# One maximum row per query, unmatched queries as a row product, the mean of V on TensorE: an attention stage rearranged

## The chip, the cores and the metric

The kernel runs on one core of one Trainium2 chip. The metric is the device time of one launch in microseconds (us). Three runs of the kernel before gave 839.99, 841.4 and 837.2 us, median 839.99. A core has five engines with a queue of instructions each: TensorE (PE: matmuls; PEld: the loads of their stationary operands, called weights here), VectorE (DVE), ScalarE (ACT), GpSimd (POOL) and SyncE (SP), which here only issues transfers (DMAs). Each works its own queue in order, and engines wait for each other by semaphores.

## The reference

Three layers follow each other: an attention in which a query sees only the keys of its own hash bucket, a gated feed-forward layer, and eight experts. The change touches the first alone, apart from the order in which the second one's first steps come.

```python
def _attn_ref(q, k, v, proj):                     # q, k, v: 2 x 8 heads x 768 x 64, proj: 64 x 6
    scale = 1.0 / np.sqrt(D)
    q_bits = (np.einsum('bhsd,dk->bhsk', q, proj) > 0)      # 6 bits: the bucket
    k_bits = (np.einsum('bhsd,dk->bhsk', k, proj) > 0)
    mask = q_bucket[:, :, :, None] == k_bucket[:, :, None, :]
    scores = scale * np.matmul(q, k.transpose(0, 1, 3, 2))
    scores = np.where(mask, scores, -1000000000.0)
    scores = scores - np.max(scores, axis=-1, keepdims=True)
    attn = np.exp(scores)
    attn = attn / (np.sum(attn, axis=-1, keepdims=True) + 1e-09)
    return np.matmul(attn, v)
# then, on 1536 tokens x 512:
#   first layer:  xn = rms_norm(x); (silu(xn @ w_gate) * (xn @ w_val)) @ w_out       (1536 hidden columns)
#   second layer: the expert of the largest logit, relu(x @ w1[e]) @ w2[e], times two gates
```

A query without any key in its bucket has 768 equal scores, so its output is the mean of V over the sequence.

## The kernel before

**Tiling.** The 16 heads are worked in 8 pairs. A pair's q and k are loaded (`load_qk`), transposed by TensorE (`prep_t`), split into a leading part and a rest (`prep_hi`, `prep_lo`), and multiplied by the projection for the bucket bits (`bits_dots`, `bits_mask`). SyncE copies these pieces inside SBUF into the operands `T` of a head (`place`: part 0 the leading parts, part 1 the bit rows, part 2 the rests). The bit rows are extra rows of the contraction: they put a penalty of 2^30 (`PEN`) on a key of another bucket.

**Per head.** The 768 queries are six tiles of 128, and so are the keys.
- `smax` (tile `psm`, L576): masked scores of 128 queries against all keys, two matmuls of 384 columns. `smax_red` (L585, VectorE) reduces them to one maximum per query.
- `setm` turns the maxima of a head into a row of `T`: to 0 where the query has no match (L597), split into a leading part and a rest (L600, L602), transposed (L605), copied out (L608), and sent into two rows of `T` by a DMA (L611). So the next product already has the maximum subtracted.
- `scores` (`pss`, L621): 128 keys against all queries, four matmuls. `exps` (L629, ScalarE) writes `Pe` in float32; `exps_lo` (L640) makes `Pl`, what is left of it beyond its upper half word, on GpSimd or, for the tiles listed in `PLV`, on VectorE.
- `pv` (`po`, L655, L656): output of 128 queries, twelve pairs of a weight load and a matmul: for each key tile the upper half of `Pe` against [leading V | 1 | rest of V | 0], 130 columns, and `Pl` against the first 65 of them. V is scaled by a power of two and split per head by `v_hi` (ScalarE) and `v_lo` (L506, VectorE).
- `pv_red` (L663, VectorE) adds the two halves of `po`; `head_out` makes the denominator (L673) and its reciprocal (L677) on VectorE and, on GpSimd, the mean of V where a query is unmatched (`u` L589, L680), the scaling (L684) and their sum (L686).

**Mean of V.** `mean_red` (L700, VectorE) adds the six tokens of a partition, `mean_dots` (L736, TensorE) the partitions; `abs_sum` (L705) and `v_scale` find the power of two.

**What sets the order.** `Plan` writes the order of every engine before the kernel starts: each step is added with an engine, a duration in ns, what it needs, a place (a number from tables such as `PT`, `SM`, `LATE`) and buffers; a model of the engines starts, of the steps that can run, the one with the least place. Two `P` (exponentials of a head) and three `S` (score tiles in PSUM) are there. The feed-forward layer has a `Plan` of its own behind it; its first norm and first weights (`n0` to `n5`, `w0`) are steps of the attention's plan.

Of the kernel before, what the change touches and what calls it, by code (L numbers as in the profile page):

```python
# [32 lines left out]
PT = ((-26.2, 3.87, 20.05, 19.0, 13.9), (-59.0, -88.6, -21.21, 8.39, 33.83), (1.61, -13.88, 4.9, -16.2, -30.33), (-0.8, -11.52, 5.11, -27.98, -8.39), (-1.86, -21.15, -8.14, -41.78, 8.93))  # L33
PD = (68.86, 49.56, -49.64, -53.27, 14.34)
SM = ((-25.22, 2.38, -4.9, 2.26), (-3.98, 1.69, 1.66, 1.07), (-2.41, 1.13, 7.87, 0.73), (-0.14, 1.24, 9.29, 0.52), (2.7, 1.02, -7.12, 11.99))
SV = (-51.83, 11.07, 7.09, 5.16, 12.58)
LQ = (3.84, 74.35, 127.92, 164.5, 49.05)
LV = (11.15, -49.62, -114.49, -63.86, -39.46)
TINY = 2.0 ** -126
TDA = (4,)  # L40
PLV = ((6, 11), (2, 11), (3, 6, 8), (4, 7), (0, 1, 3, 4, 5, 8, 9, 11))
PV0, PV1 = 10.03, 4.39
VAT = (-156.17, -11.57)
MVT = (-17.05, -173.85)
MLT = (131.86, 57.75)
NX, NW = 350.58, 20.18
CONST = 4.79
N0, N1 = 68.31, 14.5
LATE = {'tc': -15.85, 'td': 7.02, 'pr': 25.66, 'p0': -15.14, 'bi': -15.81, 'sx': 12.56, 'mk': -1.88, 'ex': 6.16, 'pl': -8.9, 'xr': 20.85, 'ho': -22.34, 'u': -63.48, 'sc': -1.81, 'sm': -2.37, 'pv': 48.28, 'vs': 27.89, 'tl': 14.99}


class Plan:
    """An order for a fixed set of steps: on each engine, of the steps that can run, the one with the least place."""
# [18 lines left out]

    def order(self):
        """Starts of the steps on a model of the engines: ns of each step, ns to its followers, buffers in use."""
# [8 lines left out]
        start, events, now, dma, done = {}, [], 0, 0, 0  # L83
# [10 lines left out]
        while True:  # L94
            for e, r in enumerate(ready):
# [10 lines left out]
                end = free[e] = now + steps[n][1]  # L106
# [33 lines left out]
def kernel(  # L140
# [85 lines left out]
    def constants():  # L226
# [6 lines left out]
        # per token: one, and the token's row of the output  # L233
# [15 lines left out]
    def x_tiles(w):  # L249
        """Leading parts and rests of w columns of activations, in two buffers by turns."""  # L250
# [7 lines left out]
    def to_psum(pt, src):  # L258
        """Token-major src [P, DM] transposed."""
# [20 lines left out]
    def norm_rsqrt(pool, d):  # L280
        """Steps from the sums of squares d["ss"] to d["ri"]: 1 / sqrt, from the exponent's bits by Newton's steps."""
# [59 lines left out]
    def convert(f, kind):  # L341
        """Steps from float64 words to float32: rebias the exponent, join the fraction's words, put the sign back."""
# [50 lines left out]
    def attention(ctx, after):  # L393
# [35 lines left out]
        MV = [tp.tile([P, DM], F32, name=f"MV{b}") for b in range(B)]  # L429
# [3 lines left out]
        VS = [tp.tile([P, 2, NT, 2, D + 1], F16, name=f"VS{i}") for i in range(2)]  # L433
        one128 = tp.tile([1, P], F32, name="one128")
# [46 lines left out]

        def ends_V(i):
# [992 lines left out]
```

## Time and profile before

| | |
|---|---|
| median of 3 runs | 839.99 us |
| span of the profiled execution (the page gives no other time of it) | 840.8 us |
| TensorE busy | 750.0 us, 89% |
| VectorE busy | 526.9 us, 63% |
| ScalarE busy | 380.7 us, 45% |
| GpSimd busy | 439.0 us, 52% |
| first and last scores start | 39.2 and 260.6 us |
| first matmul of the feed-forward layer | 273.3 us |

The span is the time from the first to the last instruction. A busy share is an average over three layers with different limits, so the stage matters: the attention fills the first 273 us, then the feed-forward layer's first chunk runs together with the conversion of its float64 weights until about 395 us, and the rest is matmuls almost without a break. An instruction of VectorE or GpSimd counts as busy also while it waits inside for a port. The granted clock of TensorE is given as a share of its 2.4 GHz.

### The profile page before, as it was taken

What the parts mean: (1) busy time and instruction counts of PE and PEld (TensorE: products, weight loads), DVE (VectorE), ACT (ScalarE), POOL (GpSimd) and SP (SyncE); (2) the same over time, 40 slices, a digit from 0 to 9 for tenths busy, and PEclk for the clock granted to TensorE, in tenths of its full rate; (3) what the DMA queues carried; (4) which work ended last, traced back from release to release, by engine and by line L of the source; (5) the groups of instructions that cost most, each with busy time, mean ns of one, the idle gap of its engine ahead of it and who ended that gap; (6) DMA issues with size and microseconds to landing.
All of it is one profiled execution on the core that took longest, in us unless ns stands there. A gap on an engine that the chain in (4) does not pass through costs nothing.

```text
span 840.8 us, 12945 instructions
## 1 busy us (share of the span) xinstructions
PE 750.0 (89%) x4722; PEld 629.8 (75%) x4722; DVE 526.9 (63%) x915; ACT 380.7 (45%) x625; POOL 439.0 (52%) x373
## 2 busy tenths in 40 slices
PE   5689898997887988879999999999987999999995
PEld 4368687876776666657878888788866888898984
DVE  5799998999998999998351222521243444455441
ACT  2066544543354544453443334434232666565662
POOL 4075676786569544444434444346116665655552
PEclk9599999999898999999999999999986999999998
DMA  7999767553501445440100001010038997767100
GB/s 148 190 227 215 166 129 154 121 120 62 137 1 51 151 155 165 143 145 18 51 1 0 1 1 51 1 38 13 1 126 256 340 334 212 220 204 188 39 23 19
DMA packets 101665, 97.03 MB, mean 115 GB/s; under 512 B 33501, under 2 KB 82845, under 8 KB 101600
## 3 DMA queue, kind: packets, MB, share of 16 engines
q1 hardware_dynamic: 98880, 88.84, 40.4%
q0 software_dynamic: 2560, 7.34, 2.5%
q8 instruction: 38, 0.62, 0.3%
q14 instruction: 27, 0.22, 0.1%
q10 hardware_dynamic: 160, 0.00, 0.0%
HBM read 69.50 MB, written 7.36 MB: 91 GB/s over the span
## 4 chain that ended last, share of the span: by engine, by line
PE 60%; DVE 29%; issue 5%; DMA 2%; SPq 1%; ACT 1%; POOL 0%; POOLq 0%; DVEq 0%; ACTq 0%
PE pg L915 16%; PE pg L1310 10%; PE pss L621 4%; DVE hm L362 4%; PE psm L576 3%; PE po L1324 3%; PE po L1323 3%; PE po L1322 3%; DVE m L585 3%; PE po L957 3%; PE po L959 3%; PE po L958 3%; PE po L655 2%; DVE Pl L640 2%; PE pt L261 1%
## 5 line engine op out<-in xcount | busy, mean ns | idle before, releaser
L640 POOL TENSOR_TENSOR Pl<-Pe 128x768 f16<-128x768 f32 x73 | 113.3, 1563 | 63.1 <-ACT Pe L629 59.1
L629 ACT ACTIVATE Pe<-pss,ebias 128x768 f32<-128x768 f32 x96 | 84.8, 902 | 109.1 <-PE pss L621 95.3
L378 POOL TENSOR_TENSOR wgl<-r,wgh 128x512 fp32r<-128x512 f32 x64 | 83.7, 1314 | 82.6 <-ACT wgh L388 80.9
L585 DVE TENSOR_REDUCE m<-psm 128x1 f32<-128x768 f32 x96 | 89.4, 948 | 14.2 <-PE psm L576 12.9
L621 PE MATMUL pss<-T 128*128 128x384 f32 x384 | 89.1, 363 | 9.3 <-DVE m L585 4.2
L937 DVE TENSOR_TENSOR si<-pg,si 128x512 f32<-128x512 f32 x36 | 24.8, 688 | 109.8 <-PE pg L915 109.8
L928 POOL TENSOR_TENSOR wgl<-wy_g,wgh 128x512 fp32r<-128x512 f32 x35 | 47.5, 1356 | 80.0 <-ACT wgh L388 80.0
L621 PEld LDWEIGHTS pss<-T 128*128 128x128 f32 x384 | 69.0, 199 | 13.5 <-DVE m L585 5.5
L378 DVE TENSOR_TENSOR wvl<-r,wvh 128x512 fp32r<-128x512 f32 x64 | 47.2, 737 | 47.9 <-ACT wvh L388 42.0
L1310 PE MATMUL pg<-xh,wgh 128*128 128x256 f32 x256 | 73.5, 288 | 0.7 <-ACT xh L264 0.7
L928 POOL TENSOR_TENSOR wol<-wy_o,woh 128x512 fp32r<-128x512 f32 x36 | 49.0, 1364 | 47.8 <-ACT woh L388 45.1
L928 POOL TENSOR_TENSOR wvl<-wy_v,wvh 128x512 fp32r<-128x512 f32 x35 | 48.1, 1375 | 49.1 <-ACT wvh L388 46.0
L1310 PE MATMUL pg<-xl,wgh 128*128 128x256 f32 x256 | 72.7, 284 | 0.0
L1310 PE MATMUL pg<-xh,wgl 128*128 128x256 f32 x256 | 72.6, 284 | 0.0
L655 PE MATMUL po<-VS,Pe 128*128 128x130 f16 x576 | 65.2, 229 | 6.1 <-DVE xr L663 5.7
L576 PE MATMUL psm<-T 128*128 128x384 f32 x192 | 58.6, 402 | 11.7 <-DMA T<-bits 7.5
L957 PE MATMUL po<-woh,hh 128*128 128x512 f32 x144 | 58.5, 406 | 5.1 <-ACT hh L945 5.0
L656 PE MATMUL po<-VS,Pl 128*128 128x65 f16 x576 | 62.2, 199 | 0.0
L655 PEld LDWEIGHTS <-Pe 128*128 128x128 bf16 x576 | 53.5, 102 | 11.6 <-issue 10.8
L959 PE MATMUL po<-woh,hl 128*128 128x512 f32 x144 | 58.0, 403 | 4.5 <-DVE hl L949 4.5
L915 PE MATMUL pg<-xh,wvh 128*128 128x512 f32 x144 | 59.9, 416 | 0.0
L1315 DVE SCALAR_TENSOR_TENSOR ehl<-pg,ehh 128x256 fp32r<-128x256 f32 x64 | 27.2, 424 | 51.8 <-ACT ehh L1314 51.8
(221 smaller groups left out, 2002.1 us busy)
## 6 DMA issues: line engine op xcount, KB each, us to landing
r<-in_moe_w_dram SPq DMA_DIRECT2D x128, 256.0 KB
T<-HL SPq DMA_DIRECT2D x48, 384.0 KB
wraw<-in_moe_w_gate_dram SPq DMA_DIRECT2D x12, 512.0 KB
wraw<-in_moe_w_val_dram SPq DMA_DIRECT2D x12, 512.0 KB
wraw<-in_moe_w_out_dram SPq DMA_DIRECT2D x12, 512.0 KB
kraw<-in_k_dram SPq DMA_DIRECT2D x16, 192.0 KB
qraw<-in_q_dram SPq DMA_DIRECT2D x16, 192.0 KB
vraw<-in_v_dram SPq DMA_DIRECT2D x16, 192.0 KB
```

The source lines that it names most:

```text
L378: eng.tensor_tensor(out=lo, in0=y, in1=r32(hi), op=ALU.subtract)
L576: nc.tensor.matmul(pm[:, hf, 0:HS], Tj[:, 0, 1, t * P:(t + 1) * P], Tj[:, 0, 0, hf * HS:(hf + 1) * HS], start=True, stop=True)
L585: v_.tensor_reduce(out=d["m", j][:, t:t + 1], in_=d.pop(("pm", n))[:, :, 0:HS], axis=AX.XY, op=ALU.max)
L621: nc.tensor.matmul(pss[:, hf, 0:HS], Tj[:, a, 0, ks], Tj[:, a, 1, qs], start=a == 0, stop=a == 1)
L629: nc.scalar.activation(d["p", j][0][:, kb], d.pop(("s", n))[:, :, 0:HS], AF.Exp, bias=ebias, scale=1.0 / math.sqrt(D))
L640: eng.tensor_tensor(out=Pl[:, kb], in0=Pe[:, kb].rearrange("p a s -> p (a s)"), in1=leading(Pe, kb), op=ALU.subtract)
L655: nc.tensor.matmul(po, leading(Pe, kb)[:, t * P:(t + 1) * P], vf, start=kb == 0, stop=False)
L915: nc.tensor.matmul(pg, w_[:, dsl], x_[:, d], start=n == 0, stop=n == 3 * KD - 1)
L928: nc.gpsimd.tensor_tensor(out=lo, in0=Y[(f, kind)], in1=r32(hi), op=ALU.subtract)
L957: nc.tensor.matmul(pos[c, t], d["hh"][:, tsl], wh, start=f == 0, stop=False)
L959: nc.tensor.matmul(pos[c, t], d["hl"][:, tsl], wh, start=False, stop=f == NF - 1)
L1310: nc.tensor.matmul(ph, w_[:, dsl], x_[:, d], start=n == 0, stop=n == 3 * KD - 1)
```

## The change

- `setm`: the maxima are transposed as they are; one copy limits them below by -PEN/2 (`mT`, one row of `T` in place of two), one writes PSC where the query has no match, else 0 (`uT`). The latter goes by two DMAs into two rows of a 128 x 768 tile `UR`, whose other rows are zero.
- `pv`: a first matmul multiplies `UR` by `VM`, which holds the mean of V in two parts in its first two rows; then, per key tile, three matmuls of 65 columns in place of one of 130 and one of 65. All six query tiles of a head lie in one PSUM bank, `pv_red` and the GpSimd steps of `head_out` go, and VectorE scales straight from PSUM.
- The mean of V: six float32 matmuls per batch on TensorE, then four steps on ScalarE and VectorE to `VM`.
- `v_hi`, `v_lo`: once per pair of heads.
- `PLV`: VectorE makes 6 of the 96 `Pl`, all in the last pair (before: 23). `TDA`: in the first pair too the rests of q and k come from TensorE and ScalarE (before: in the last alone).
- `Plan`: new durations and places, and a `lock`: steps marked with it on VectorE and all of GpSimd's exclude each other in the model.

```diff
-        NR = MR + 2
+        NR = MR + 1
...
         def setm(i, j, step):
-            # the maximum of a row with a match, else 0
             d = st[i]
             if step == 0:
-                m = d["m", j]
-                d["mk", j] = wk.tile([P, NT], F32, name="mk")
-                v_.scalar_tensor_tensor(out=d["mk", j], in0=m, scalar=-PEN / 2, in1=m, op0=ALU.is_gt, op1=ALU.mult)
...
+                d["pT", j] = ps_v.tile([P, 512], F32, name="pT", tag=plan.tag("V"))
+                nc.tensor.transpose(d["pT", j][0:NT, 0:P], d["m", j], ident)
             elif step == 1:
...
+                d["mT", j] = wk.tile([NT, P], F32R, name="mT")
+                v_.tensor_scalar(out=d["mT", j], in0=d["pT", j][0:NT, 0:P], scalar1=-PEN / 2, scalar2=None, op0=ALU.max)
             elif step == 2:
...
+                v_.tensor_scalar(out=d["uT", j], in0=d["pT", j][0:NT, 0:P], scalar1=-PEN / 2, scalar2=PSC,
+                                 op0=ALU.is_le, op1=ALU.mult)
             elif step == 3:
...
+                nc.sync.dma_start(r32(T[i % TB][j][r0:r0 + 1, 0, 1]), r32(d["mT", j]))
             else:
+                for r in range(2):
+                    nc.sync.dma_start(d["ur", j][r:r + 1], d["uT", j])
...
         def pv(i, j, t):
...
+            nc.tensor.matmul(po, d["ur", j][:, ts], VM[b][:, 2 * hp + j], start=True, stop=False)
             for kb in range(NT):
-                vf = VS[i % 2][:, j, kb].rearrange("p c d -> p (c d)")
-                nc.tensor.matmul(po, leading(Pe, kb)[:, t * P:(t + 1) * P], vf, start=kb == 0, stop=False)
-                nc.tensor.matmul(po[:, D + 1:W], Pl[:, kb, t * P:(t + 1) * P], vf[:, 0:D + 1],
-                                 start=False, stop=kb == NT - 1)
-
-        def pv_red(i, j, g):
...
+                vf = VS[i % 2][:, j, kb]
+                nc.tensor.matmul(po, leading(Pe, kb)[:, ts], vf[:, 0], start=False, stop=False)
+                nc.tensor.matmul(po, leading(Pe, kb)[:, ts], vf[:, 1], start=False, stop=False)
+                nc.tensor.matmul(po, Pl[:, kb, ts], vf[:, 0], start=False, stop=kb == NT - 1)
...
-            elif step == 3:
-                nc.gpsimd.tensor_tensor(out=xs, in0=d["xr", j][:, :, 0:D], in1=d["rd", j].to_broadcast([P, NT, D]), op=ALU.mult)
             else:
-                nc.gpsimd.tensor_tensor(out=xs, in0=xs, in1=d["um", j], op=ALU.add)
+                v_.tensor_tensor(out=X[b][:, :, h * D:(h + 1) * D], in0=po[:, :, 0:D],
+                                 in1=d["rd", j].to_broadcast([P, NT, D]), op=ALU.mult)
...
-            nc.tensor.matmul(st[b]["pmv"], meanc, MV[b], start=True, stop=True)
+            vall = X[b].rearrange("p t c -> p (t c)").rearrange("p (h t d) -> p t h d", h=H, t=NT)
+            for t in range(NT):
+                nc.tensor.matmul(st[b]["pmv"].rearrange("p (h d) -> p h d", h=H), meanc, vall[:, t], start=t == 0, stop=t == NT - 1)
...
-TDA = (4,)
-PLV = ((6, 11), (2, 11), (3, 6, 8), (4, 7), (0, 1, 3, 4, 5, 8, 9, 11))
+TDA = (0, 4)
+PLV = ((), (), (), (), (0, 2, 4, 6, 8, 10))
```

The order moves everywhere; three places matter to the prediction.

VectorE in the middle of the attention, one head of a steady pair, before (`m` a maximum, `xr` the sum of the two halves of `po`, `HL` the rests of q or k):

```order
L597 SCALAR_TENSOR_TENSOR mk<-m 128x6
L663 TENSOR_REDUCE xr<-po 128x195
L600 CAST ms<-mk 128x6
L673 TENSOR_SCALAR den<-xr,vsc_130 128x6
L602 TENSOR_TENSOR ms<-mk,ms 128x6
L677 RECIPROCAL rd<-den 128x6
L506 SCALAR_TENSOR_TENSOR VS_125<-vraw,vsc_131,VS_125 128x6x64
L608 CAST mT<-pT 12x128
L585 TENSOR_REDUCE m<-psm 128x1
L535 TENSOR_TENSOR HL<-pt,HL 128x768
L663 TENSOR_REDUCE xr<-po 128x195
```

The same place in the changed kernel:

```order
L600 TENSOR_REDUCE m<-psm 128x1 x9
L610 TENSOR_SCALAR mT<-pT 6x128
L675 TENSOR_SCALAR den<-po,vsc_134 128x6
L614 TENSOR_SCALAR uT<-pT 6x128
L521 SCALAR_TENSOR_TENSOR VS_123<-vraw,vsc_135,VS_123 128x12x64
L600 TENSOR_REDUCE m<-psm 128x1
L679 RECIPROCAL rd<-den 128x6
L681 TENSOR_TENSOR X_71<-po,rd 128x6x64
L600 TENSOR_REDUCE m<-psm 128x1 x2
L550 TENSOR_TENSOR HL<-pt,HL 128x768
```

The steps on 128x6 tiles in SBUF before the transpose and the reductions of `po` are gone; `den` reads PSUM; the scaling to `X` is VectorE's.

TensorE at the start, before (`T_121`, `T_122` are the two heads of the first pair, `T_123`, `T_124` of the second):

```order
L576 MATMUL psm<-T_121 128x384 x12
L576 MATMUL psm<-T_122 128x384 x12
L605 MATMUL pT<-ident,ms 12x128
L576 MATMUL psm<-T_123 128x384 x6
L621 MATMUL pss<-T_121 128x384 x4
L576 MATMUL psm<-T_123 128x384 x2
L621 MATMUL pss<-T_121 128x384 x4
```

The same place in the changed kernel (`T_119` and `T_120` the first pair, `T_121` and `T_122` the second):

```order
L591 MATMUL psm<-T_120 128x384 x6
L528 MATMUL pt<-ident,kraw 128x128 x6
L591 MATMUL psm<-T_122 128x384 x2
L591 MATMUL psm<-T_121 128x384 x2
L607 MATMUL pT<-ident,m 6x128
L591 MATMUL psm<-T_122 128x384 x2
L591 MATMUL psm<-T_121 128x384 x6
L591 MATMUL psm<-T_122 128x384 x2
L591 MATMUL psm<-T_121 128x384 x2
L631 MATMUL pss<-T_119 128x384 x24
```

The first scores stand behind eight maximum products of the second pair (16 matmuls) in place of three (6).

SyncE in the middle, the copies into the second head's operands, before (`bits` the bit rows, `mT` the maxima):

```order
L611 DMA T_121<-mT 2x6x128
L560 DMA T_124<-HL 64x1536
L566 DMA T_124<-bits 14x768 x2
L568 DMA T_124<-HL 64x2x768
L569 DMA T_124<-HL 64x2x768
```

The same place in the changed kernel:

```order
L618 DMA T_121<-mT 1x6x128
L511 DMA vraw<-in_v_dram 128x384 x2
L581 DMA T_120<-bits 13x768 x2
L583 DMA T_120<-HL 64x2x768
L584 DMA T_120<-HL 64x2x768
L575 DMA T_120<-HL 64x1536
```

The copy of the leading parts (L560, now L575), which the maximum products need beside the bit rows, stood first and stands last.

## Rows read from the trace of the kernel before

**Rows 1.** Windows: length; busy (count) of PE, PEld, DVE, ACT, POOL; clock, DMA, GB/s

```profile
39.20:260.60 221.40, 191.74 (x1755) 165.71 (x1755) 207.72 (x312) 113.76 (x150) 152.89 (x125) 0.95 0.58 130
...
273.30:395.00 121.70, 104.50 (x413) 80.62 (x411) 119.81 (x189) 55.65 (x93) 54.85 (x42) 0.92 0.43 134
```

**Rows 2.** Source L621, the scores: ns min/median/max, first and last start

```profile
L621 PE MATMUL pss<-T x384: 331/338/688, 39.2 to 260.6; 128*128 128x384 f32 x192
```

**Rows 3.** Waits, 39.2 to 260.6 us: us in total, times, longest

```profile
ACT Pe L629 <- PE pss L621: 95.3, 53, 24.7
```

**Rows 4.** Lines by form, 0 to 276 us: busy us, mean ns, idle before

```profile
L640 POOL TENSOR_TENSOR Pl<-Pe 128x768 f16<-128x768 f32 x73 | 113.3, 1563 | 63.1 <-ACT Pe L629 59.1 <-PE po L656 3.8
L640 DVE TENSOR_TENSOR Pl<-Pe 128x768 f16<-128x768 f32 x23 | 27.3, 1204 | 0.4 <-ACT Pe L629 0.4
L506 DVE SCALAR_TENSOR_TENSOR VS<-vraw,vsc,VS 128x384 f16<-128x384 f32 x16 | 18.7, 1173 | 0.4 <-ACT VS L502 0.4
...
L663 DVE TENSOR_REDUCE xr<-po 128x195 f32<-128x390 f32 x32 | 17.6, 552 | 3.2 <-POOL um L680 1.7 <-PE po L656 1.5
...
L673 DVE TENSOR_SCALAR den<-xr,vsc 128x6 f32<-128x6 f32 x16 | 12.8, 797 | 0.0
L700 DVE TENSOR_REDUCE MV<-X 128x128 f32<-128x768 f32 x8 | 11.6, 1517 | 0.0
L602 DVE TENSOR_TENSOR ms<-mk,ms 128x6 fp32r<-128x6 f32 x16 | 7.5, 470 | 0.0
L597 DVE SCALAR_TENSOR_TENSOR mk<-m 128x6 f32<-128x6 f32 x16 | 6.9, 430 | 0.0
...
L608 DVE CAST mT<-pT 12x128 fp32r<-12x128 f32 x16 | 4.3, 267 | 1.2 <-PE pT L605 1.1
L268 DVE TENSOR_TENSOR xl<-nt,xh 128x512 fp32r<-128x512 f32 x4 | 2.7, 679 | 0.7 <-ACT xh L264 0.7
```

**Rows 5.** Sources L673 and L506, ns min/median/max

```profile
L673 DVE TENSOR_SCALAR den<-xr,vsc x16: 217/740/1506, 77.6 to 274.1; 128x6 f32<-128x6 f32 x16
...
L506 DVE SCALAR_TENSOR_TENSOR VS<-vraw,vsc,VS x16: 600/1140/1901, 65.2 to 232.4; 128x384 f16<-128x384 f32 x16
```

**Rows 6.** Timeline of TensorE, 149.3 to 151.5 us: start, length, instruction

```profile
149.39 0.23 PE L655 MATMUL po<-VS,Pe 128*128 128x130 f16 x1
149.46 0.19 PE L656 MATMUL po<-VS,Pl 128*128 128x65 f16 x1
149.49 0.22 PE L655 MATMUL po<-VS,Pe 128*128 128x130 f16 x1
...
149.93 0.59 PE L576 MATMUL psm<-T 128*128 128x384 f32 x2
150.36 0.85 PE L621 MATMUL pss<-T 128*128 128x384 f32 x4
151.05 0.51 PE L576 MATMUL psm<-T 128*128 128x384 f32 x2
151.40 0.23 PE L655 MATMUL po<-VS,Pe 128*128 128x130 f16 x1
```

**Rows 7.** Timeline of TensorE: a pair's transposes (one of two), its bit products

```profile
155.28 0.85 PE L513 MATMUL pt<-ident,kraw 128*128 128x128 f32 x6
...
166.29 2.28 PE L545 MATMUL pd<-HL,PRJ 128*64 128x384 f32 x12
```

**Rows 8.** Timeline of TensorE, 430 us: eight short matmuls with a weight load each

```profile
430.48 0.36 PE L1056 MATMUL pdp<-movi,ohr 128*128 128x16 f16 x8
430.69 0.47 PE L957 MATMUL po<-woh,hh 128*128 128x512 f32 x1
```

**Rows 9.** Chain that ended last, 50 to 90 us: one mean product

```profile
59.87 1.12 PE pmv L736 x2
```

**Rows 10.** Timeline at the start: SyncE's queue, TensorE's wait, a maximum

```profile
8.43 0.64 SPq L240 DMA_DIRECT2D rw<-n_moe_w_output_gate_dram  x1
...
37.13 2.26 PE L576 MATMUL psm<-T 128*128 128x384 f32 x6 [5.96 <-DMA T<-bits]
...
38.22 0.96 DVE L585 TENSOR_REDUCE m<-psm 128x1 f32<-128x768 f32 x1 [5.01 <-PE psm L576]
```

More of the change, by code (lines that the diff above doesn't have):

```diff
@@ L58, in __init__, with add @@
         self.room, self.steps, self.at, self.slots, self.now = room, [], {}, {}, None
-    def add(self, eng, ns, key, fn, args=(), needs=(), place=0.0, take="", give="", bw=0):
+    def add(self, eng, ns, key, fn, args=(), needs=(), place=0.0, take="", give="", bw=0, lock=False):
         self.at[key] = len(self.steps)
         place += LATE.get(key[0], 0.0)
-        self.steps.append((eng, ns, fn, args, needs, place, take.split(), give.split(), bw))
+        self.steps.append((eng, ns, fn, args, needs, place, take.split(), give.split(), bw, lock or eng == POOL))
     def taker(self, n, buf):
@@ L82, in order @@
         free = [0] * len(self.WAIT)
-        start, events, now, dma, done = {}, [], 0, 0, 0
+        start, events, now, dma, done, lock = {}, [], 0, 0, 0, 0
         def release(n):
@@ L105, in order @@
                 start[n] = now
-                end = free[e] = now + steps[n][1]
+                begin = now
+                if steps[n][9]:
+                    begin = max(now, lock)
+                    lock = begin + steps[n][1]
+                end = free[e] = begin + steps[n][1]
                 if steps[n][8]:
@@ L641, in exps_lo @@
                               op=ALU.subtract)
-        W = 2 * (D + 1)
-        TG = 3
         def pv(i, j, t):
@@ L787, in attention @@
                     ("", "V", "", "", "", "V", "")[m], ("", "", "V", "", "", "", "V")[m])
[L788 to L789 removed]
+            add(PE, 5400, ("mvm", b), mean_dots, (b,), [("mvl", b), ("vx", b, 6), "const"], MVT[b] + 6, "V")
+            for m, (e, ns) in enumerate(((ACT, 680), (DVE, 690), (ACT, 650), (DVE, 1000))):
+                add(e, ns, ("mr", b, m), mean_rows, (b, m), [("mr", b, m - 1)] if m else [("mvm", b)], MVT[b] + 6,
+                    "", "V" if m == 1 else "", lock=m == 3)
         for i in range(len(pairs)):
@@ L820, in attention @@
+            add(DVE, 1000, ("vs", i, 1), v_lo, (i,), (("vs", i, 0),), pr, lock=True)
             for j in range(2):
@@ L842, in attention @@
-                    e, ns = (DVE, 870) if x in PLV[n] else (POOL, 1600)
-                    add(e, ns, ("pl", i, x), exps_lo, (i, x), (("ex", i, x),), t0 + x)
-                ready = [("pl", i, NT * j + m) for m in range(NT)] + [("vs", i, j, e) for e in range(2)]
+                    add(PE, 700, ("sc", i, x), scores, (i, x), [("mk", i, j, 3), ("d2", i, j)], t0 + x, "S")
+                    add(ACT, 902, ("ex", i, x), exps, (i, x), [("sc", i, x)] + [("ex", i, NT * j)] * (m > 0), t0 + x, "P" if m == 0 else "", "S")
@@ L856, in attention @@
-                add(POOL, 960, ("ho", i, j, 3), head_out, (i, j, 3), [("ho", i, j, 1)] + [("mv", b, g) for g in range(4)], pr, "", "XR")
-                add(POOL, 960, ("ho", i, j, 4), head_out, (i, j, 4), [("ho", i, j, 3), ("ho", i, j, 2)], pr, "", "UM")
-        done = [("ho", i, j, 4) for i in range(HP) for j in range(2)]
+                    add(PE, 600, ("pv", i, j, m), pv, (i, j, m), [("pv", i, j, m - 1)] if m else ready, pr,
+                        "" if m else "V", "P U" if m == NT - 1 else "")
@@ L859, in attention @@
+                for m, ns in enumerate((220, 182, 540)):
+                    add(DVE, ns, ("ho", i, j, m), head_out, (i, j, m), [("ho", i, j, m - 1)] if m else [("pv", i, j, NT - 1)] + [("mvm", b)] * (m == 2), pr,
+                        "", "V" if m == 2 else "")
+        done = [("ho", i, j, 2) for i in range(HP) for j in range(2)]
         steps = norm_rsqrt(wk, n0)
         for i in range(CT):
-            add(DVE, 600, ("n0", i), norm0_sum, (i,), done, N0 + N1 * i, "J", "J")
+            add(DVE, 760, ("n0", i), norm0_sum, (i,), done, N0 + N1 * i, "J", "J", lock=True)
@@ L862, in attention @@
         for n, f in enumerate(steps):
-            add(DVE, 70, ("n1", n), f, (), [("n1", n - 1)] if n else [("n0", i) for i in range(CT)], N0 + N1 * CT)
+            add(DVE, 163, ("n1", n), f, (), [("n1", n - 1)] if n else [("n0", i) for i in range(CT)], N0 + N1 * CT, lock=True)
         for i in range(CT):
             pr = N0 + N1 * (CT + 1 + i)
-            add(DVE, 660, ("n2", i), lambda i: norm_scale(0, i, n0["ri"]), (i,), ("load", ("n1", len(steps) - 1)), pr)
-            add(PE, 430, ("n3", i), norm0_t, (i,), (("n2", i),), pr, "V")
```

216 lines of the change are left out of this document (102 added, 114 removed).

## The prediction

> **What bounds the kernel now.** I read the windows by stage first, then the waits inside the first stage, then the lines by form, and last TensorE's timeline for what a single step takes. The scores run from 39.2 to 260.6 us [rows 2], and in that stretch VectorE is busy 207.72 of 221.40 us, 94% [rows 1]. TensorE has 191.74 us, 87%, and GpSimd 152.89 us, 69%. ScalarE waits 95.3 us for scores [rows 3] and so has room. VectorE is the nearest to full, and TensorE not far behind: whatever comes off VectorE is worth at most the distance to TensorE. From 273.3 to 395 us VectorE is full again, 119.81 of 121.70 us [rows 1], with the weight conversion, which the change leaves alone. So a gain in the attention can't grow there, and one that is made before 273.3 us is kept.
>
> **VectorE's account** [rows 4, 5]. Off: the sums of `po`'s halves (L663), 17.6 us; `mk` and the rest of the maximum (L597, L602), 6.9 + 7.5 = 14.4; `mean_red` (L700), 11.6; 17 of its 23 `Pl`, 17 x 1.204 = 20.5. `den` took 797 ns in the mean, 217 at the least, on 128x6 elements; the excess is waiting inside. If reading PSUM ends that, 16 x 0.58 = 9.3 us go, otherwise none. `v_lo` becomes 8 calls of twice the size: between 8 x 1.20 = 9.6 (the fastest, 600 ns, doubled) and the 18.7 us of before; I take 5 off. Together 78.4.
> On: `uT`, 16 copies like L608, 16 x 0.267 = 4.3. The scaling from PSUM, 16 instructions of 384 columns; no row has it, so bounds from a 552 ns reduction of PSUM (L663) and from 679 ns for 512 columns of two operands (L268): 8.8 to 10.9, taken 10. The steps that make the rows of the mean, twice in the whole; no row has them, so bounds from a 0.27 us copy and a 1.52 us reduction (L700), two of each kind at most per batch: 1 to 6, taken 4. Together 18.3.
> Net -60 us: 207.7 becomes about 148 of 200. VectorE has slack then, and none of the unknown sizes here decides anything. GpSimd gets 17 x 1.563 = 26.6 us of `Pl` (73 were 113.3, so 90 are 141) and loses the steps of `u` and `head_out`: about 70% of the stretch still. TensorE must be next.
>
> **TensorE's account.** Unhindered, at the full clock, steps follow each other so [rows 6]: from the first value product at 149.39 to the next step at 149.93, 0.54 us for twelve pairs of load and matmul; a maximum product 0.35 to 0.43, taken 0.39; scores 0.69. Transposes take 0.85 for each of q and k, the bit products 2.28 [rows 7]. Between the first and the last scores lie 96 scores (66.2 us), 81 of 96 maximum products (31.6; 15 stand ahead of the first scores), 85 of 96 value steps (45.9; 11 lie behind the last scores), six pairs' preparation (6 x (1.70 + 2.28) = 23.9), and two mean products at 1.12 (2.2) [rows 9]. That is 170 us of work, against 191.74 that the profile counts as busy; the difference is the tail that each instruction's busy time has beyond the start of the next, and a clock of 0.95 [rows 1].
> The change makes the twelve pairs nineteen, all of 65 columns. In rows 6 the 130-column matmul is followed by the 65-column one after 70 ns, that by the next after 30 ns: together 100 ns a key tile, where only one 65-column spacing is seen. Is 30 ns the spacing behind every 65-column matmul? Eight pairs of 16 columns fill 0.21 us, 26 ns each [rows 8], so an unhindered pair of load and matmul can be that short. By 30 ns a step is 19 x 0.03 = 0.57 us: 85 x 0.57 = 48.5, +2.6 us in all. The mean products become six per batch, 12 x 1.12 = 13.4, +11.2. So 170 becomes 184, +14.
>
> **A rule against this.** The Trainium skill, page "TensorE: Matmul & The Clock Gate", section "Back-to-back issue gap", says that in a stream of load and matmul pairs the spacing is set by both operations, some 81 ns at 128 columns. By it a step of 19 pairs would take an estimated 1.54 us. This case's trace disagrees with 70, 30 and 26 ns [rows 6, 8], and the sum goes by the trace.
>
> **The stretch.** TensorE becomes its limit. If it is kept as full as VectorE was, 94%, the 184 us take 196. If what the profile counts as busy is all real and nothing fills it up, 191.7 + 14 = 206. I take the middle, 201: -20.4 us against 221.4.
>
> **The start.** The first scores stand behind eight maximum products of the second pair in place of three, five more. Each frees its buffer with a reduction of 0.96 us [rows 10], so 5 x 0.96 = +4.8. The copies of the router's weights, 0.64 us each on SyncE's queue [rows 10], stand ahead of the first loads of k: two, +1.2. Together +6. The work isn't lost wholly, since those five maximum products are missing later, but I have VectorE's slack cover them there. Bounds: 0, if the first scores wait for the copies in either case (the first maximum product waited 5.96 us for the bit rows [rows 10]), and +11, if the six mean products of the first batch (6 x 1.12 = 6.7 less what they cover) also hold up the first value product, which now needs `VM`.
>
> **The end.** Behind the last scores now come the last head's scaling, without GpSimd's steps, but also the first norm, whose four rests (L268, 4 x 679 ns = 2.7) move behind the last `Pl`. I take +2; bounds 0 and +6, the latter with the norm's scaling and transposes in sequence on top.
>
> **Moved and cheap.** SyncE copies the leading parts last. Were the maximum products waiting for that, each pair would lose a copy; yet VectorE and TensorE have a whole pair of work between, so I take 0, up to the start's bound. The two row copies of `uT` per head have a head's time until the value products: 0. The `lock` exists in the model alone.
>
> **Sum.** Profiled span 840.8 + 6 - 20.4 + 2 = 828.4; the median of the runs is 0.8 below that span, so 827.6, given as 828. About 0.5%, 4.2 us, is what a measurement of this kernel can tell from no change: faster means below 835.8, slower above 844.2.
>
> **Rivals.**
> 1. *TensorE was already the bound and its busy time is real.* Its busy 191.7 us would include whatever the array can't avoid; with 14 more it is 206, and at 97% full the stretch takes 212, -9. With +8 for start and end: 839. For it: TensorE's 87%, and a clock below full in the stretch [rows 1]. Against it: unhindered steps sum to 170, not 191. Chance 0.10.
> 2. *Slower: every pair of load and matmul has a floor.* Twelve pairs in 0.54 us are 45 ns each; if that is the price of a pair whatever its columns, nineteen cost 0.85 us, 0.28 more than I have, x 85 = +24 on 201, and the sum gives 852. It decides from about 40 ns a pair on: 16.6 us more than my sum are needed to reach 844.2, 16.6 / (85 x 19) = 10 ns. For it: the step's 0.54 is all that the trace shows of the kind. Against it: 26 and 30 ns [rows 6, 8]. Chance 0.11.
> 3. *Better: TensorE filled to the brim.* With VectorE slack and three score buffers, its 184 us at 97% take 190, and start and end cost nothing: 840.8 - 31.4 = 809. For it: nothing else is above 75% then. Against it: heads wait for maxima, row copies and exponentials in a chain, and the clock has been at 0.95. Chance 0.18.
> That the change leaves VectorE on the path, since its instructions wait longer inside beside GpSimd's 17 more `Pl`, is not a case of its own: were half of the -60 us lost so, VectorE would have 178 us, and TensorE's 184 would still be the more.
>
> **Numbers.** Forecast 828, chance 0.61; its own range 818 to 836, from the stretch's 196 and 206 and the bounds of start and end taken partly together. Faster: nearly all of the forecast (0.60) and rival 3, in sum 0.78. Slower: rival 2, 0.11. The same: rival 1 and the forecast's upper edge, 0.11. The range takes rival 3's time and rival 1's, 807 to 843; rival 2 and the far ends are left out.
>
> **What would show it.** In the profile after: VectorE's share between first and last scores falls from 94% to about 74% and TensorE's rises to 92% or more; the first scores start near 45 us and the last near 246; a value step runs from its first matmul to the next step in 0.57 us; the chain that ended last goes through TensorE, not VectorE, there; the first feed-forward matmul comes near 261 us, and what follows it is as long as before. I am wrong in the mechanism if a value step takes 0.85 us, if VectorE stays above 90%, or if TensorE idles more than 10% of the stretch waiting for copies or `Pl`.

## The result and the profile after

The changed kernel takes 829.2 us (median of 4 runs, 827.97 to 831.26), against 840.69 us for the kernel before beside it: a ratio of 0.9862, with a 95% interval of 0.9831 to 0.9893. Forecast were 828 us. The profiled execution has a span of 829.6 us, 11.2 less than before; the medians differ by 11.5. A profile shows one execution, here one of 831.26 us, 2.1 above the median, so where two profiles are compared below, the medians stand beside them. The marks of the profile tell where the gain lies. First the first scores and the first matmul of the feed-forward layer, as the views by source line give them (durations in ns, then the first and last start):

```profile
L631 PE MATMUL pss<-T x384: 331/337/690, 44.4 to 253.7; 128*128 128x384 f32 x192
...
L920 PE MATMUL pg<-xh,wgh x144: 388/392/628, 266.3 to 597.0; 128*128 128x512 f32 x144
```

| part | before | after | difference | forecast |
|---|---|---|---|---|
| to the first scores | 39.2 | 44.4 | +5.2 | +6 |
| first to last scores | 221.4 | 209.3 | -12.1 | -20.4 |
| last scores to the first feed-forward matmul | 12.7 | 12.6 | -0.1 | +2 |
| from there to the end | 567.5 | 563.3 | -4.2 | 0 |

So the sum came out right, but its terms did not: the stretch between the scores is 8.3 us longer than forecast, the rest together 7.1 us shorter, 4.2 of them behind the first feed-forward matmul.

The windows of after, with the columns of [rows 1]: between the scores, and from the first feed-forward matmul to the transposes of the next chunk.

```profile
44.40:253.70 209.30, 193.78 (x2338) 168.47 (x2337) 147.03 (x225) 111.00 (x141) 134.15 (x88) 0.96 0.62 135
266.30:373.95 107.65, 91.61 (x360) 69.79 (x361) 106.81 (x165) 52.72 (x88) 45.22 (x31) 0.94 0.49 152
```

VectorE went from 207.72 to 147.03 us in the stretch (forecast 148), 70% of it, TensorE to 92.6%. The lines by form of VectorE show the account item by item (columns as in [rows 4]):

```profile
L650 DVE TENSOR_TENSOR Pl<-Pe 128x768 f16<-128x768 f32 x6 | 11.0, 1858 | 0.5 <-ACT Pe L639 0.5
L521 DVE SCALAR_TENSOR_TENSOR VS<-vraw,vsc,VS 128x768 f16<-128x768 f32 x8 | 10.2, 1280 | 1.3 <-ACT VS L518 1.0
L681 DVE TENSOR_TENSOR X<-po,rd 128x384 f32<-128x384 f32 x16 | 8.7, 549 | 0.2
...
L614 DVE TENSOR_SCALAR uT<-pT 6x128 f16<-6x128 f32 x16 | 4.3, 270 | 2.7 <-DMA UR<-uT 2.7
L675 DVE TENSOR_SCALAR den<-po,vsc 128x6 f32<-128x6 f32 x16 | 3.4, 214 | 4.9 <-PE po L666 4.7
```

`uT` took 4.3 us as forecast, the scaling 8.7 (10), `v_lo` 10.2 in place of 18.7 (5 off were taken, 8.5 went), and the denominator 214 ns each from PSUM against 797 from SBUF [rows 4, 5]. The six `Pl` that VectorE kept took 1858 ns each, 11.0 us in place of the 7.2 that the forecast's 1204 ns would make; with VectorE at 70% that decided nothing.

What TensorE waits for has another name now. Waits in the stretch, of before and of after (engine, line, what it waits for, us in total, times, longest):

```profile
PE pT L605 <- DVE ms L602: 11.0, 7, 3.2
PE pss L621 <- DVE m L585: 4.2, 5, 2.3
PE pmv L736 <- DVE MV L700: 3.9, 2, 2.0
PE pss L621 <- DVE bits L550: 3.9, 1, 3.9
```

```profile
PE psm L591 <- DMA T<-HL: 5.2, 3, 2.8
PE pss L631 <- DMA T<-mT: 2.7, 2, 2.5
PE psm L591 <- issue: 1.9, 1, 1.9
PE po L661 <- DVE uT L614: 1.8, 1, 1.8
```

Adding up the starts of TensorE's timeline in the stretch, each instruction up to the next one's start, waits apart: before, 191.9 us of work and 29.5 of waits, 28.6 of them for VectorE; after, 193.7 of work and 15.5 of waits, 4.0 for VectorE and 8.4 for copies. That is the gain of 12.1: 14.0 us of waits went, 1.9 us of work came. Behind the 1.9 stand +4.1 for the value steps and +7.5 for the mean products (9.5 after 2.0), less 3.8 for scores, 2.1 for maximum products (five fewer fall into the stretch), 2.4 for transposes of the first norm (now behind it) and 1.5 of smaller differences. A value step on the timeline of after (start, length, instruction):

```profile
143.39 0.20 PE L661 MATMUL po<-VM,UR 128*128 128x65 f16 x1
143.43 0.20 PE L664 MATMUL po<-VS,Pe 128*128 128x65 f16 x1
143.47 0.19 PE L665 MATMUL po<-VS,Pe 128*128 128x65 f16 x1
143.50 0.19 PE L666 MATMUL po<-VS,Pl 128*128 128x65 f16 x1
...
143.99 0.94 PE L591 MATMUL psm<-T 128*128 128x384 f32 x4
```

Nineteen pairs from 143.39 to 143.99: 0.60 us, 32 ns each, where 0.57 was forecast.

### The profile page after: what moved, and what is told of

It is laid out like the page before. It is cut to its first block, busy times and chain, and to the rows that moved or that the text cites. A ratio compares the mean times of both kernels' runs of the same rounds, so it can differ in the third digit from the quotient of the medians.

```text
span 829.6 us, 14253 instructions
## 1 busy us (share of the span) xinstructions
PE 756.4 (91%) x5418; PEld 634.6 (76%) x5418; DVE 467.7 (56%) x838; ACT 381.3 (46%) x621; POOL 412.2 (50%) x330
## 4 chain that ended last, share of the span: by engine, by line
PE 47%; DVE 14%; issue 3%; ACT 1%; DMA 0%; POOL 0%; POOLq 0%; DVEq 0%; ACTq 0%
PE pg L920 16%; PE pg L1315 10%; DVE hm L368 4%; PE po L1329 3%; PE po L1328 3%; PE po L1327 3%; PE po L962 3%; PE po L964 3%; PE po L963 3%; PE pt L267 1%; PE po L989 1%; DVE wy_v L376 1%; DVE wy_g L376 1%; DVE wy_o L376 1%; DVE si L942 1%
## 5 line engine op out<-in xcount | busy, mean ns | idle before, releaser
L650 POOL TENSOR_TENSOR Pl<-Pe 128x768 f16<-128x768 f32 x90 | 138.5, 1566 | 106.3 <-ACT Pe L639 106.2
L639 ACT ACTIVATE Pe<-pss,ebias 128x768 f32<-128x768 f32 x96 | 82.7, 902 | 82.2 <-PE pss L631 60.0
L631 PE MATMUL pss<-T 128*128 128x384 f32 x384 | 84.0, 355 | 2.7 <-DMA T<-mT 2.7
L664 PE MATMUL po<-VS,Pe 128*128 128x65 f16 x576 | 63.3, 195 | 0.0
L665 PE MATMUL po<-VS,Pe 128*128 128x65 f16 x576 | 63.3, 197 | 0.0
L394 ACT CAST wgh<-r 128x512 fp32r<-128x512 f32 x64 | 39.7, 620 | 42.3 <-PE pg L1315 29.8
```

What stands on the lines that cost most here:

```text
L631: nc.tensor.matmul(pss[:, hf, 0:HS], Tj[:, a, 0, ks], Tj[:, a, 1, qs], start=a == 0, stop=a == 1)
L639: nc.scalar.activation(d["p", j][0][:, kb], d.pop(("s", n))[:, :, 0:HS], AF.Exp, bias=ebias, scale=1.0 / math.sqrt(D))
L650: eng.tensor_tensor(out=Pl[:, kb], in0=Pe[:, kb].rearrange("p a s -> p (a s)"), in1=leading(Pe, kb), op=ALU.subtract)
L664: nc.tensor.matmul(po, leading(Pe, kb)[:, ts], vf[:, 0], start=False, stop=False)
L665: nc.tensor.matmul(po, leading(Pe, kb)[:, ts], vf[:, 1], start=False, stop=False)
```

## The experiments

Experiments are of the changed kernel unless the text says otherwise. "First" is the first matmul of the feed-forward layer in the profiled execution.

| kernel | median us | before beside it | ratio (95% interval) | scores from, to | first |
|---|---|---|---|---|---|
| changed | 829.2 | 840.69 | 0.9862 (0.9831 to 0.9893) | 44.4, 253.7 | 266.3 |
| e1 row product x7 | 835.07 | 841.89 | 0.9937 (0.9905 to 0.9969) | 45.2, 254.9 | 268.9 |
| e2 no rest of V | 826.32 | 841.89 | 0.9801 (0.9778 to 0.9824) | 44.7, 253.6 | 266.8 |
| e3 maxima x2, 30 us | 841.37 | 841.89 | 0.9998 (0.9981 to 1.0014) | 51.4, 264.0 | 276.5 |
| e4 maxima x2, 61 us | 862.84 | 841.89 | 1.0237 (1.0213 to 1.026) | 57.2, 284.9 | 297.5 |
| e5 place of the copy | 869.49 | 841.56 | 1.0337 (1.0308 to 1.0366) | 45.1, 292.8 | 302.5 |
| e6 no copies to `UR` | 830.18 | 841.56 | 0.9866 (0.9823 to 0.9909) | 44.6, 251.7 | 264.3 |
| e7 before, value part alone | 843.61 | 841.56 | 1.0021 (1.0003 to 1.004) | 39.9, 271.7 | 274.0 |
| e8 old places | 834.37 | 841.56 | 0.9927 (0.9906 to 0.9949) | 41.1, 253.9 | 268.1 |
| e9 copy swapped | 821.41 | 839.97 | 0.9791 (0.9757 to 0.9826) | 45.4, 242.9 | 255.5 |
| e10 more copies | 846.99 | 839.97 | 1.0095 (1.0058 to 1.0133) | 44.8, 267.6 | 280.2 |
| e11 e9 and row product x7 | 836.23 | 839.97 | 0.9947 (0.9926 to 0.9968) | 44.9, 258.8 | 272.8 |
| e12 e9, mean on VectorE | 857.03 | 841.24 | 1.0188 (1.0165 to 1.0211) | 44.7, 272.4 | 286.6 |

**Is TensorE the bound? (e1, e2)**

```diff
-            nc.tensor.matmul(po, d["ur", j][:, ts], VM[b][:, 2 * hp + j], start=True, stop=False)
+            for n in range(7):
+                nc.tensor.matmul(po, d["ur", j][:, ts], VM[b][:, 2 * hp + j], start=n == 0, stop=False)
```

> The row product is issued seven times in place of once per value step (an unmatched query's numerator and denominator both grow by seven, so the output stays); the order of all steps is the same. It adds 6 x 96 = 576 pairs of load and matmul on TensorE, at the 31 ns of spacing seen in the changed kernel about 18 us. Theory (TensorE is now the bound of the attention): +14 to +20, 843 to 849 us. Rival (TensorE's 15.5 us of idle time between the scores, in which it waits for copies, takes it up): +5 at most, below 834 us.

```diff
-                nc.tensor.matmul(po, leading(Pe, kb)[:, ts], vf[:, 1], start=False, stop=False)
```

> The products of the leading exponentials with the rest of V are left out (the output lacks that small part); same order of steps. 576 pairs less on TensorE, about -18 us of its work. Theory (TensorE is the bound): -12 to -18, 811 to 817 us. Rival (the chain of maxima, row copies, exponentials and Pl sets the pace): -5 at most, above 824 us.

The windows between first and last scores, of e1 and of e2:

```profile
45.20:254.90 209.70, 203.94 (x2848) 180.01 (x2847) 144.36 (x225) 111.27 (x141) 133.67 (x89) 0.99 0.61 135
```

```profile
44.70:253.60 208.90, 184.99 (x1827) 154.39 (x1827) 145.63 (x225) 109.96 (x141) 134.57 (x88) 0.94 0.62 135
```

209.7 and 208.9 us, against 209.3. TensorE was busy 204 us in the one and 185 in the other, and in these executions the stretch stayed. The medians move a little: e1 lost some 6 us and e2 won 3 (medians) to 5 (ratios), about a third of the 18 us at most. e2's profiled execution took 832.78 us, 6.5 more than its median, so its window may hide a part of its gain. e1's 835.07 us lies just above the rival's 834 and 8 us below the theory; e2 lies where the rival put it. In e1 the waits for the leading parts sank from 5.2 to 0.7 us; in e2, with less to do, they grew (the first line is e1's, the others e2's):

```profile
PE psm L591 <- DMA T<-HL: 0.7, 2, 0.5
...
PE psm L591 <- DMA T<-HL: 6.2, 3, 2.8
PE psm L591 <- DVE bits L565: 3.1, 1, 3.1
PE psm L591 <- DMA UR<-uT: 2.9, 1, 2.9
```

So most of the added work went into waits that TensorE had anyway: from start to start its work grew by 10.3 us in e1 and its waits shrank by 9.8. TensorE at 92.6% was not what set the pace, or at most for a third; something else did.

**Has VectorE room? (e3, e4)**

```diff
-            v_.tensor_reduce(out=d["m", j][:, t:t + 1], in_=d.pop(("pm", n))[:, :, 0:HS], axis=AX.XY, op=ALU.max)
+            pm = d.pop(("pm", n))
+            for _ in range(2 if t < 2 else 1):         # e4: t < 4
+                v_.tensor_reduce(out=d["m", j][:, t:t + 1], in_=pm[:, :, 0:HS], axis=AX.XY, op=ALU.max)
```

> VectorE makes the maxima of query tiles 0 and 1 of every head twice (same result, same order of steps): 32 x 0.949 = +30 us of VectorE work. Theory (VectorE has about 60 us of slack): +8 at most, below 837 us, from the maxima that come later in a head's chain. Rival (VectorE is still on the path everywhere): +20 to +30, above 849 us.

> The same for query tiles 0 to 3: 64 x 0.949 = +61 us on VectorE, about what the change took off it. Theory (the relief of VectorE is where the gain comes from): VectorE has 205 us between first and last scores and is the bound again, 205 / 0.94 = 218 us, the stretch +9 or more: 838 to 850 us, the gain is gone. Rival (the gain comes from the new order and not from VectorE's load): below 835 us.

The windows between the scores, of e3 and of e4:

```profile
51.40:264.00 212.60, 192.90 (x2338) 166.31 (x2337) 167.87 (x249) 111.22 (x141) 135.49 (x88) 0.98 0.58 127
```

```profile
57.20:284.90 227.70, 200.95 (x2336) 168.62 (x2337) 186.91 (x275) 111.40 (x141) 136.82 (x88) 0.96 0.52 115
```

21 us more on VectorE in the stretch (168 after 147) made it 3.3 us longer; another 7.0 us of e3 are the start, where the doubled maxima stand ahead of the first scores. 19 us more (187) made it another 15 longer, and TensorE waits for maxima again; ahead of the maximum products of e4:

```profile
PE psm L591 <- DVE m L602: 13.2, 20, 1.9
```

The slack is there, but it ends at about 80% of the stretch. e3 lies between its theory and its rival, nearer to the theory; e4 is slower than its theory said and refutes its rival. VectorE off TensorE's path is thus a condition of the gain. Whether its load does it or the time to a head's maxima is not shown: a doubled maximum adds to both, and in e4 VectorE is busy 82% of the stretch, not the 94% of before.

**What it is not (e6), and a part alone (e7)**

```diff
             else:
-                for r in range(2):
-                    nc.sync.dma_start(d["ur", j][r:r + 1], d["uT", j])
+                pass
```

> The two copies per head of the unmatched row into UR are left out (32 issues; UR stays zero, so unmatched queries lose their mean); same order of steps. They take 34 us of SyncE's queue between the first and last scores. Theory (SyncE's queue paces the copies): -4 to -10, 819 to 825 us. Rival (SyncE, busy 143 of 209 us, has room; my cost of 0): within 2 us of 829.

830.18 us, ratio 0.9866: no change. The time of SyncE's queue as such is not the bound. For e7 the kernel before got three products of 65 columns into one bank, without the sums:

```diff
-                nc.tensor.matmul(po, leading(Pe, kb)[:, t * P:(t + 1) * P], vf, start=kb == 0, stop=False)
-                nc.tensor.matmul(po[:, D + 1:W], Pl[:, kb, t * P:(t + 1) * P], vf[:, 0:D + 1],
-                                 start=False, stop=kb == NT - 1)
+                nc.tensor.matmul(po, leading(Pe, kb)[:, ts], vf[:, 0], start=kb == 0, stop=False)
+                nc.tensor.matmul(po, leading(Pe, kb)[:, ts], vf[:, 1], start=False, stop=False)
+                nc.tensor.matmul(po, Pl[:, kb, ts], vf[:, 0], start=False, stop=kb == NT - 1)
...
-                nc.gpsimd.tensor_tensor(out=xs, in0=d["xr", j][:, :, 0:D], in1=d["rd", j].to_broadcast([P, NT, D]), op=ALU.mult)
+                v_.tensor_tensor(out=xs, in0=d["po", j][:, :, 0:D], in1=d["rd", j].to_broadcast([P, NT, D]), op=ALU.mult)
```

> The kernel before with one part alone: three products of 65 columns into one bank, no sums of halves, the denominator and the scaling by VectorE from PSUM; GpSimd still adds the mean. VectorE loses 17.6 + 9.3 and gets some 9 us, -18 net; TensorE gets about 4 us. Theory (VectorE was the bound, one us of it costs about one): -10 to -18, 823 to 831 us. Rival (the gain needs the new order or the other parts): above 836 us.

843.61 us: a miss for the theory. VectorE's own time sank only from 207.72 to 201 us, over a longer stretch:

```profile
39.90:271.70 231.80, 202.17 (x2355) 173.57 (x2355) 201.24 (x305) 114.49 (x153) 149.58 (x117) 0.94 0.57 128
```

The planner ordered everything anew with places that were found for other steps, and put the last scores later. One part gives nothing by itself here; which of the parts give the gain together isn't settled.

**Operations or places? (e8)** All tables of places and `LATE` are those of before (one of the lines):

```diff
-PD = (-426.28, 114.86, 211.04, -423.7, 949.39)
+PD = (68.86, 49.56, -49.64, -53.27, 14.34)
```

> The changed kernel's operations with the places of before (PT, PD, SM, SV, LQ, LV, PV0, PV1, VAT, MVT, MLT, NX, NW, CONST, N0, N1, LATE); TDA, PLV, durations and lock stay new. Theory (the operations, by what they take off VectorE, make the gain): 826 to 834 us. Rival (the new places make it): above 837 us.

834.37 us, ratio 0.9927 against 0.9862: about half of the gain is left with the old places. The result lies just above what the theory expected; the other half came with the new places.

**The copies (e5, e9, e10, e11).** e5 was a blunt edit:

```diff
-PD = (-426.28, 114.86, 211.04, -423.7, 949.39)
+PD = (-426.28, 114.86, 211.04, -1000.0, -1000.0)
```

> From the fourth pair on, the copy of the leading parts gets a lower place, so that SyncE issues it ahead of the bit rows and the rests as before the change; nothing else is edited, the rest of the order follows. Since the stretch between first and last scores stayed at 209 us with 18 us more or 17 us less on TensorE, something else paces it. Theory (the copies: the leading parts, which every maximum product needs, land last): TensorE's 5.2 us of waits for them go, -4 to -8, 821 to 825 us. Rival (another loop paces it): within 2 us of the changed kernel's 829.

869.49 us, far outside both. The whole order followed: SyncE issued nothing between 134.4 and 146.4 us, since a pair's loads had come behind steps of TensorE, and the time is that of another order, not of the copy. The question had to be put without the planner. On the timelines of the changed kernel one sees the loop that was to be tested. SyncE's queue (start, time in the queue, line, what is copied):

```profile
95.35 1.63 SPq L581 DMA_DIRECT2D T<-bits  x2
...
123.53 1.61 SPq L581 DMA_DIRECT2D T<-bits  x2
...
149.31 1.62 SPq L581 DMA_DIRECT2D T<-bits  x2
151.04 0.68 SPq L583 DMA_DIRECT2D T<-HL  x1
151.81 0.66 SPq L584 DMA_DIRECT2D T<-HL  x1
152.52 1.34 SPq L575 DMA_DIRECT2D T<-HL  x1
...
158.70 1.67 SPq L581 DMA_DIRECT2D T<-bits  x2
...
161.89 1.43 SPq L575 DMA_DIRECT2D T<-HL  x1
...
179.25 1.64 SPq L581 DMA_DIRECT2D T<-bits  x2
```

TensorE in the same time:

```profile
166.60 0.88 PE L631 MATMUL pss<-T 128*128 128x384 f32 x4
170.33 0.98 PE L591 MATMUL psm<-T 128*128 128x384 f32 x2 [2.85 <-DMA T<-HL]
172.19 1.63 PE L591 MATMUL psm<-T 128*128 128x384 f32 x4
...
176.36 0.94 PE L631 MATMUL pss<-T 128*128 128x384 f32 x4
...
178.52 0.88 PE L631 MATMUL pss<-T 128*128 128x384 f32 x4
```

Read it as a circle. The copies into a head's operands need all six scores of the head that used them two pairs earlier. A head's last scores free them (178.52 and 0.7 us after), and at 179.25 SyncE issues the bit rows of a later pair into them, two copies of the rests, and the leading parts last; the same once more for the other head. The leading parts of the second head are issued at 161.89 and land at 170.33, after 2.5 MB that were issued from 149.31 on (by the profile's sizes: five copies of 384 KB, 384 KB of V and the bit rows). There TensorE's queue stands at a maximum product that needs them; behind it, in order, stand the last two scores of the head whose operands are to be freed next. This turn took 29.9 us (149.31 to 179.25), the two before it 25.8 and 28.2 (from 123.53 and from 95.35), while a pair is some 24.3 us of work for TensorE (12 scores at 0.69, 12 maximum products at 0.40, 12 value steps at 0.60, 4.0 of preparation). In e9 only the copy of the leading parts moves, on SyncE's queue, after all has been ordered:

```diff
-        for n in self.order():
+        seq = self.order()
+        for k in [k for k in self.at if k[0] == "d0" and k[1] > 1]:
+            seq.remove(self.at[k])
+            seq.insert(seq.index(self.at[("d1", *k[1:])]), self.at[k])
+        for n in seq:
```

> From the third pair on, the copy of the leading parts is written directly ahead of the copy of the bit rows of the same head on SyncE's queue; no other step moves on any engine (in e5_lead_first the whole order followed, and that run says little of the copy). Theory (a loop paces the stretch: a head's last scores free its operands, the copies fill them, the leading parts land last, TensorE's queue stands at a maximum product that waits for them, and behind it stand the last scores of the other head): the leading parts no longer stand behind two copies of 384 KB, 2 to 4 us a pair over five pairs, -6 to -16: 813 to 823 us. Rival (the copies are not in the loop): within 2 us of 829.

```diff
                 nc.sync.dma_start(t[oth, 1], hl[src, 0:3:2])
+                nc.sync.dma_start(scr, hl[:, 0, 0:512]) if i > 1 else None
```

> From the third pair on, one more copy of 256 KB inside SBUF per head, into a tile that nobody reads, behind the copies of the rests and ahead of the leading parts; all other steps as in the changed kernel. At 195 GB/s it is about 1.3 us, 2.6 a pair. Theory (the loop through the copies): +8 to +20 over the stretch, 837 to 849 us. Rival (copies are hidden beside TensorE): +3 at most, below 832 us.

821.41 and 846.99 us: the theory held both times. Against the changed kernel, e9 is 6 us faster by the ratios and 8 by the medians, and e10 18 to 20 slower, for twelve copies of 256 KB. e10's waits for the leading parts grew to 10.1 us; it delays other transfers too (4.2 us of waits for q, which the changed kernel hasn't), so that it is e9 that singles out the leading parts. In e9 no wait for them is left, and the three turns take 24.6, 24.3 and 24.6 us:

```profile
97.23 0.55 SPq L575 DMA_DIRECT2D T<-HL  x1
...
121.83 0.54 SPq L575 DMA_DIRECT2D T<-HL  x1
...
146.09 0.54 SPq L575 DMA_DIRECT2D T<-HL  x1
146.73 1.96 SPq L581 DMA_DIRECT2D T<-bits  x2
...
170.70 0.54 SPq L575 DMA_DIRECT2D T<-HL  x1
```

```profile
45.40:242.90 197.50, 189.02 (x2338) 165.40 (x2337) 146.50 (x225) 110.73 (x141) 134.91 (x88) 0.98 0.65 143
```

```profile
PE psm L592 <- DMA T<-HL: 10.1, 3, 3.7
```

(The last is e10's.) The stretch of e9 is 197.5 us, and TensorE is busy 96% of it. Of the 11.8 us less, 7.1 are waits, and 4.7 are the same work done faster, at a clock of 0.98 after 0.96. The medians differ by less than the profiles: e9's profiled execution took 820.02 us, 1.4 less than its median, that of the changed kernel 2.1 more. e11 asks whether TensorE is the bound then; its edit is that of e9 and e1 together.

> e9_lead_swap with the row product seven times, as in e1_row7 (+18 us on TensorE, output the same). If the swap takes the copies out of the loop and TensorE is next, its 18 us now cost: 8 to 18 us above e9_lead_swap. If another loop holds, or the copies still do, within 5 us of e9_lead_swap.

```profile
44.90:258.80 213.90, 204.17 (x2847) 179.87 (x2847) 143.79 (x225) 111.12 (x141) 133.17 (x89) 0.98 0.61 132
```

836.23 us, 13 (ratios) to 15 (medians) above e9: the theory held. The stretch grew by 16.4, which is rather too much, since e11's profiled execution took 839.0 us, 2.8 more than its median. The same edit that cost some 6 us in e1 costs 13 to 15 of its 18 here.

**A last attempt (e12).** The six float32 products of the mean go back to sums on VectorE and one product:

```diff
-            for t in range(NT):
-                nc.tensor.matmul(st[b]["pmv"].rearrange("p (h d) -> p h d", h=H), meanc, vall[:, t], start=t == 0, stop=t == NT - 1)
+            nc.tensor.matmul(st[b]["pmv"].rearrange("p (n w) -> p n w", n=2), meanc, rows_tile()[:, b, :, DM // 2:DM], start=True, stop=True)
...
+            for n in range(4):
+                add(DVE, 1500, ("mv", b, n), mean_red, (b, n), (("mvl", b),), MVT[b] + 2 * n)
```

> e9_lead_swap with one part of the change undone: VectorE adds the six tokens of a partition again (8 reductions of about 1.5 us, +12 us of VectorE, into parts of the tile of the mean rows), TensorE does one float32 product per batch (the two means took 9.5 us between first and last scores, the one 2.0 before the change: -7.5). The planner orders the steps anew with the same places. Theory (with the swap TensorE is the bound and VectorE, 146.5 of 197.5 us, has room): -4 to -8 against e9_lead_swap, 813 to 818 us. Rival (the new order or VectorE's lateness in the first head takes it back): within 2 us of e9_lead_swap or slower.

857.03 us, 33 (ratios) to 36 (medians) more than e9: a miss. On VectorE's timeline four sums stand ahead of the rests that TensorE's bit products need:

```profile
53.03 5.62 DVE L702 TENSOR_REDUCE MR<-X 128x128 f32<-128x768 f32 x4 [0.62 <-DMA X<-in_v_dram]
58.56 0.95 DVE L550 TENSOR_TENSOR HL<-pt,HL 128x768 fp32r<-128x768 f32 x1
```

```profile
59.57 4.10 PE L560 MATMUL pd<-HL,PRJ 128*64 128x384 f32 x12 [6.48 <-DVE HL L550]
```

TensorE waited 13.0 us in two places for that. The order of everything else changed too, so that the 36 us are not shown to be the mean's alone. e9 is the fastest version: 0.9791 of before (0.9757 to 0.9826).

## Why the prediction came out right, and where it was wrong

- *VectorE is what the stretch gains from.* Right: 147.0 us against 148, TensorE's waits for it fell from 28.6 to 4.0 us, and e4 gives the gain back. Open are the share of each part, of which e7 tried one, and that of the new places, without which half of the gain is gone (e8).
- *The start, +6.* +5.2. The first scores stand at 44.4 as forecast, near 45. Nearly all of it is the five maximum products more: in both kernels the last group of them ahead of the scores starts near 37.2 us, and takes 2.1 us before and 7.2 after. The router's copies, taken at +1.2, left 0.1 there.
- *A value step of 19 pairs, 0.57 us.* 0.60 us; rival 2 with its floor of 45 ns a pair is out. The Trainium skill, page "TensorE: Matmul & The Clock Gate", section "Back-to-back issue gap", gives some 81 ns a pair at 128 columns. Carried over to pairs of 65 columns, as in the prediction's estimate of 1.54 us, it is far too much: they follow at about 31 ns here.
- *The mean products, +11.2.* +7.5: twelve instructions of a batch took 5.3 us in a row, not 6.7, since the 1.12 us of [rows 9] run to the end of a product and the next one starts before that.
- *"What the profile counts as busy" has a tail that isn't work.* Wrong as to the tail; in this rival 1 was right. Work counted from start to start was 191.9 us before, the same as the busy time; what the 170 us of unhindered work lacked were slower stretches (scores took 0.81 us in the mean, 78.1 us for 96, and not 0.69, at the clock of 0.95 that the prediction names too) and 4.2 us of small products left out of the sum.
- *TensorE becomes the limit of the stretch, 201 us.* This step failed, though TensorE's share came out as forecast. e1 and e2 move its work by 18 us either way and the medians by 6 us at most. Busy at 92.6% was no proof of a bound. None of the prediction's signs of a wrong mechanism showed it: a value step took 0.60 us, VectorE stood at 70%, and TensorE waited 8.4 us for copies, 4% of the stretch, where the sign asked for 10%.
- *The copies' order, "I take 0".* This is the term that was mis-sized. The prediction argued that VectorE and TensorE have a whole pair of work between; but a maximum product that waits holds up the scores behind it, and those hold the operands that the next copy needs. It cost 6 to 8 us by ratios and medians; the two profiled stretches, 209.3 and 197.5 in e9, differ by 11.8. Without it the stretch lies inside the 196 to 206 that the prediction gave, and TensorE is nearly the limit (13 to 15 of 18 us in e11).
- *The copies of `uT`, 0.* Right (e6).
- *The end, +2.* -0.1.
- *Nothing gains behind 273.3 us.* Wrong by 4.2 us, which made up for half of the miss in the stretch.

The last point in rows: before, the window from the first feed-forward matmul to the transposes of the next chunk was

```profile
273.30:384.50 111.20, 94.00 (x365) 71.92 (x363) 109.76 (x169) 52.81 (x88) 49.76 (x39) 0.91 0.47 147
```

and it is 107.65 us after. VectorE is busy 99% of both, and has 109.76 and 106.81 us to do there: a part of one weight tile's conversion is now done ahead of it, and the last head's sum and denominator are gone. The other 0.6 us lie later. That was read from the two traces, and no run isolates it; e8 and e9 keep most of it (564.5 and 562.8 us from that matmul to the end of the profiled span), e7, where VectorE still has 201 us in its stretch, doesn't (568.6).

So the forecast of 828 was met by 829 with one large miss and several small ones of the other sign: that they cancel is luck.

## What to carry to other kernels

When an engine is relieved, look at the queue of the next one for an instruction that waits for a transfer, and ask what stands behind it and whether that frees the buffer the next transfer goes into: such a circle has a period of its own, which neither engine's busy share shows. A busy share of 93% isn't yet a bound; double or drop a little work in place, with the order kept, and see whether the time follows, by medians and not by one profile. Where a planner sets the order, an edit of its numbers or steps tests the planner (e5, e7, e12); move the one instruction behind it instead (e9).

## What was not expected of the hardware

In one place of the changed kernel TensorE pays for a wait twice. Two windows, around the wait that ends at 170.3 us:

```profile
166.60:170.30 3.70, 0.88 (x5) 0.56 (x5) 1.09 (x2) 0.90 (x1) 2.79 (x2) 0.86 1.00 206
170.30:176.30 6.00, 5.97 (x63) 5.08 (x64) 3.35 (x4) 0.00 (x0) 0.00 (x0) 0.52 0.20 44
```

After 2.85 us of waiting, the 6 us that follow have a granted clock of 0.52, the lower of the two levels of 1.2 and 2.4 GHz, and a maximum product takes 0.98 us there, as against 0.51 to 0.62 at the full clock. Not every wait is followed by that: in e1 one of 2.0 us, ending at 77.0 us, left the clock at 1.0. In e1, where the waits were filled, the clock of the stretch was 0.99, in e2 0.94: more work on TensorE ran at a higher clock, which is one reason why 18 us of it went unseen.

And the denominator, 128x6 elements on VectorE, took 202 to 227 ns from PSUM in all 16 cases, where it had taken 217 to 1506 ns from SBUF [rows 5]. Two other things changed with it, the GpSimd steps beside it and the order. e7 keeps the old places and nearly all of GpSimd's work (149.58 us in its stretch, after 152.89 before), and its 16 denominators from PSUM took 201 to 226 ns; that speaks for PSUM, though one GpSimd step is gone there too.
